# Chunked attention with a router: V in runs of two rows, pipeline units of four heads by half a sequence, bf16 turns, earlier q and k

## The chip, the cores and the metric

The kernel runs on one core of a Trainium2 chip. The metric is the device time of one execution in microseconds; lower is better. The core's engines are TensorE (PE in the profile; its weight loads are PEld), VectorE (DVE), ScalarE (ACT), GpSimd (POOL) and SyncE (SP). Each works through its own instructions in order, and semaphores tie them together. Sixteen DMA engines move data between the device memory, where the inputs lie, and the on-chip memory (SBUF). TensorE writes its results to a second on-chip memory (PSUM), from which DVE and ACT read them.

## The reference

Two parts are computed in a row. First attention over chunks of 32 queries. Each chunk sees 16 keys to its left, its own 32 and 8 to its right (56 in all), and 8 memory keys of its head: 64 columns.

```python
batch, n_heads, seq, head_dim = (4, 8, 768, 64)     # q, k, v: float32
...
for c in range(nc):                                  # nc = 768 // 32 = 24
    l_start = max(0, c_start - left_ctx); r_end = min(S, c_end + right_ctx)
    k_full = np.concatenate([mem_k, k[:, :, l_start:r_end]], axis=2)
    v_full = np.concatenate([mem_v, v[:, :, l_start:r_end]], axis=2)
    scores = scale * np.matmul(q_c, k_full.transpose(0, 1, 3, 2))
    a = np.exp(scores - np.max(scores, axis=-1, keepdims=True))
    a = a / (np.sum(a, axis=-1, keepdims=True) + 1e-09)
    out[:, :, c_start:c_end] = np.matmul(a, v_full)
```

The output, as 3072 rows of 512, goes through a mixture of 8 experts. Noisy logits choose two experts for each row, and each expert is a ReLU layer of 512 x 1024 x 512.

```python
noisy_logits = x @ w_gate + np.log1p(np.exp(x @ w_noise)) * noise
top2 = np.argpartition(-noisy_logits, 2, axis=1)[:, :2]
...
h = np.maximum(x[mask] @ w1[e], 0.0)
out[mask] += top2_w[mask, k, None] * (h @ w2[e])
```

## The kernel before

**Tiling.** The 32 heads are taken in 8 groups of four (`GP` = 2 pairs), and a group in two pipeline units. A unit is one pair of heads over the whole sequence of 768, that is six blocks of 128 queries (`BT` = 6); there are 16 units (`NPAIR`).

**Loads.** `load_qk` (L104) brings q and k of a group to SBUF and casts them to bf16. A partition holds six neighbouring rows of each head. `load_v` (L111) brings V already cut into windows: partition j of a head's half holds row j of every chunk's window, so that one piece of the transfer is one row of 64 values. The two heads of a pair lie in the upper and lower 64 partitions and in different columns of `vg`, with zeros elsewhere, which DVE writes first (L130). All these transfers are issued on POOL's queue. There are three buffers of each kind. Memory V goes straight into `memv` (L165), whose extra columns of ones make the row sums.

**A unit's steps.** `qkT_pe` (L206) turns q and k, so that the head dimension lies on the partitions: 12 + 12 matmuls against an identity into four float32 tiles in PSUM, and four ACT copies (L218) that put the rows back in order. `scores_pe` (L223) makes 12 matmuls with the memory keys (L230), 48 with the chunk windows (L240) and 4 that fill what lies beyond the sequence's ends (L243). `max_dve` and `sub_dve` (L249, L254) take the maximum and subtract it on DVE, and ACT takes the exponential (L258). `PT_pe` and `PT_dve` turn the probabilities (L265, L270). `PV_pe` (L273) multiplies them with `memv` (6 matmuls, L279) and with the windows of V (24, L282). `mult_dve` divides by the row sums (L293, L294) into `xrow`. `xT_pe` (L303, L305) turns the result, and `logits_pe` (L313) forms the router's logits.

**Order.** The order of the instructions on each engine is the order of the code. In iteration i of the main loop (L462) stand the P turns of unit i-1, logits of i-3, the maximum of i, turns of q and k of i+2, the P copy of i-1, subtraction and exponential of i, P·V of i-1, scores of i+1, the division of i-1 and the x turns of i-2. After these come the loads of the group two ahead, in every second iteration, and one step of the routing (`route`, L320) of a finished batch, which is mostly DVE work. A step of it writes the batch's rows to device memory (L385) from one of two `xrow` buffers. The first expert weights are loaded on POOL's queue in iteration 11.

**PSUM.** The turned q, k, P and x share three PSUM tiles of one tag (`tr`); the scores, the P·V result and the logits have their own.

After attention, indices are made, rows gathered in buckets of 128, and the experts run (L644, L652) to the end.

Of the kernel before, what the change touches and what calls it, by code (L numbers as in the profile page):

```python
# [12 lines left out]
F32 = mybir.dt.float32  # L13
# [11 lines left out]
def kernel(  # L25
# [28 lines left out]
    WIN = left_ctx + chunk + right_ctx  # L54
    CTX = WIN + n_mem
    SJ = S // 128
    assert D == 64 and CTX == 64 and 4 * chunk == 128 and S == 128 * SJ
# [17 lines left out]
    xd_part = dram_disjoint_views(xd, B + 1)  # L75
# [8 lines left out]
    def body():  # L84
# [12 lines left out]
        vbufs = [ap_.tile([128, GP, ncnk, 2, D], BF16, name=f"vg{i}", bufs=1) for i in range(3)]  # L97
# [13 lines left out]
        def load_v(g, i=None):  # L111
            vg = groups[g][2]
            for x in range(GP) if i is None else (i,):
                for hh in range(2):
                    p0, hd = 64 * hh, 2 * (GP * g + x) + hh

                    def piece(c, n, j=0, nj=WIN):
                        nc.gpsimd.dma_start(  # L118
                            out=vg[p0 + j:p0 + j + nj, x, c:c + n, hh, :],
                            in_=bass.AP(v.tensor, v.offset + (hd * S + c * chunk + j - left_ctx) * D, [[D, nj], [chunk * D, n], [1, D]]))  # L120

                    first, last = hd == 0, hd == B * H - 1
                    if first:
                        piece(0, 1, left_ctx, WIN - left_ctx)
                    if last:
                        piece(ncnk - 1, 1, 0, WIN - right_ctx)
                    piece(int(first), ncnk - first - last)
# [22 lines left out]
        for b in range(B):  # L150
            nc.scalar.dma_start(out=mk_nat[b * n_mem:(b + 1) * n_mem], in_=mem_k[b].rearrange("h m d -> m h d"))
        wgn_f = rp.tile([128, KP, 2, E], F32, name="wgn_f")
# [5 lines left out]
        OW = D + 2  # L158
        memv = ap_.tile([128, NPAIR, 2, OW], BF16, name="memv", bufs=1)
        nc.vector.memset(memv, 0.0)  # L160
        for hh in range(2):
            nc.vector.memset(memv[64 * hh:64 * hh + 64, :, hh, D:D + 1], 1.0)
        load_qk(0, 1)
        for hh in range(2):
            nc.gpsimd.dma_start(  # L165
                out=memv[64 * hh + WIN:64 * hh + CTX, :, hh, 0:D],
                in_=bass.AP(mem_v.tensor, mem_v.offset + hh * n_mem * D, [[D, n_mem], [2 * n_mem * D, NPAIR], [1, D]]))
        load_v(0, 1)
# [29 lines left out]
        for hp in range(HP):  # L198
            nc.tensor.transpose(out=p_m[:, hp, :], in_=mk_nat[:, 2 * hp:2 * hp + 2, :].rearrange("p h d -> p (h d)"), identity=ident)
# [6 lines left out]
        def qkT_pe(n):  # L206
            g, i = divmod(n, GP)
            qg, kg, _ = groups[g]
            SH = SJ // 2
            for nm, src in (("qT", qg), ("kT", kg)):  # L210
                dst = ap_.tile([128, 128, SJ], BF16, name=nm, bufs=3)
                for x in range(2):
                    p_t = psT.tile([128, SH, 128], F32, name="p_t", tag="tr")
                    for j in range(SH):
                        for hh in range(2):
                            nc.tensor.matmul(out=p_t[64 * hh:64 * hh + 64, j, :], lhsT=src[:, 2 * i + hh, (SH * x + j) * D:(SH * x + j + 1) * D],  # L216
                                             rhs=identb, start=True, stop=True)
                    nc.scalar.copy(dst[:, :, SH * x:SH * (x + 1)], p_t.rearrange("d j p -> d p j"))  # L218
                st[n][nm] = dst.rearrange("d p j -> d (p j)")

        UB = BT // 2

        def scores_pe(n):  # L223
            b, hp = divmod(n, HP)
            qT, kT = st[n]["qT"], st[n]["kT"]
            ps = psS.tile([128, 2, 512], F32, name="ps_s")
            for u in range(BT):
                for hh in range(2):
                    hs = slice(64 * hh, 64 * hh + 64)
                    nc.tensor.matmul(out=ps[:, hh, u * CTX + WIN:(u + 1) * CTX], lhsT=qT[hs, 128 * u:128 * (u + 1)],  # L230
                                     rhs=mkT[hs, hp, b * n_mem:(b + 1) * n_mem], start=True, stop=True)
            for c in range(ncnk):
                u, r = divmod(c, 4)
                for hh in range(2):
                    hs = slice(64 * hh, 64 * hh + 64)
                    lo = left_ctx if c == 0 else 0
                    hi = WIN - right_ctx if c == ncnk - 1 else WIN
                    k0 = chunk * c - left_ctx
                    o = ps[32 * r:32 * r + 32, hh, u * CTX:u * CTX + WIN]
                    nc.tensor.matmul(out=o[:, lo:hi], lhsT=qT[hs, chunk * c:chunk * (c + 1)], rhs=kT[hs, k0 + lo:k0 + hi], start=True, stop=True)  # L240
                    for a, z in ((0, lo), (hi, WIN)):
                        if z > a:
                            nc.tensor.matmul(out=o[:, a:z], lhsT=onesb[hs, :chunk], rhs=neg[hs, :z - a], start=True, stop=True)  # L243
# [571 lines left out]
```

## Time and profile before

| | |
|---|---|
| median of 3 runs | 388.63 us (386.53 to 389.42) |
| span of the profiled execution | 393.1 us |
| the profiled execution's own time beside that span | not given separately |
| instructions | 9217 |
| PE busy | 304.5 us (77%), 4042 matmuls, 4060 weight loads |
| DVE busy | 169.9 us (43%) |
| ACT busy | 119.8 us (30%) |
| POOL busy | 124.5 us (32%) |
| DMA | 83324 packets, 42.93 MB written |

The profile is of one execution. Its span runs from the first to the last instruction and is 4.5 us above the median of the runs. A busy share is an average over the whole span. Attention, routing and experts have different limits, so the stretches are read one by one. In the chain of work that ended last, each step is traced back to what released it. "Issue" there is time in which an engine waited for nothing that the profile shows. In the view by stretches, the columns after the stretch are its length, the busy time of each engine with its number of instructions, the granted share of TensorE's clock, the busy share of the DMA engines, and GB/s written.

### The profile page before, as it was taken

The page shows a single profiled execution, that of the slowest core. Times are in us where ns is not written, and L with a number is a line of the kernel's source. Part 1 is how long each engine was busy: PE and PEld are TensorE (multiplying, and loading weights), DVE is VectorE, ACT ScalarE, POOL GpSimd, SP SyncE. Part 2 cuts the span into 40 slices and gives each one's busy share as a digit, 9 for nine tenths or more (in the row PEclk, how much of TensorE's full clock was granted, in tenths as well). Part 3 has the DMA queues.
Part 4 walks back from the last instruction along what each step waited for, and adds up shares of the span by engine and source line. Part 5 has one row for each costly group of instructions (what it writes and reads, how often), then busy time and mean ns, then how long its engine had stood idle before and what let it go on. Part 6 is the DMA issues. An engine that isn't in the chain of part 4 may idle for free.

```text
span 393.1 us, 9217 instructions
## 1 busy us (share of the span) xinstructions
PE 304.5 (77%) x4042; PEld 188.6 (48%) x4060; DVE 169.9 (43%) x350; ACT 119.8 (30%) x235; POOL 124.5 (32%) x143
## 2 busy tenths in 40 slices
PE   0448688676846433888998998999998999999990
PEld 0436566454634322654465474454454454544540
DVE  7426345787757761342142242241433242443340
ACT  1436354565532200222333232233221312302200
POOL 7766234265000026352100420520605123032061
PEclk9999555898885655699999999999999999999997
DMA  9999999999970412849700291291492921811021
GB/s 92 100 164 156 158 152 94 167 150 141 211 154 3 143 46 80 151 82 216 141 0 2 45 221 30 64 209 34 97 213 88 191 56 71 132 67 70 3 115 59
DMA packets 83324, 42.93 MB, mean 109 GB/s; under 512 B 57255, under 2 KB 76711, under 8 KB 83280
## 3 DMA queue, kind: packets, MB, share of 16 engines
q0 software_dynamic: 74928, 38.85, 70.6%
q1 hardware_dynamic: 8064, 3.38, 3.4%
q8 instruction: 34, 0.56, 0.6%
q10 hardware_dynamic: 288, 0.07, 0.1%
q14 instruction: 10, 0.08, 0.1%
HBM read 61.32 MB, written 10.65 MB: 183 GB/s over the span
## 4 chain that ended last, share of the span: by engine, by line
PE 60%; DVE 15%; issue 10%; DMA 7%; ACT 3%; POOL 3%; POOLq 0%; DVEq 0%; ACTq 0%
PE ps_h L644 24%; PE ps_y L652 21%; DMA x_rows<-xrow 4%; PE p_t L216 3%; DMA kg<-in_k_dram 2%; PE ps_o L279 2%; PE ps_o L282 2%; DVE xrow L294 2%; PE p_t L589 2%; DVE vg L130 2%; DVE xTb L590 2%; POOL out_dram L660 2%; DVE mx L251 1%; ACT qT L218 1%; PE p_x L303 1%
## 5 line engine op out<-in xcount | busy, mean ns | idle before, releaser
L644 PE MATMUL ps_h<-xTb,w1t 128*128 128x512 bf16 (+3 forms) x608 | 107.8, 328 | 1.1 <-DVE xTb L590 1.0
L652 PE MATMUL ps_y<-w2t,ht 128*128 128x512 bf16 x430 | 98.9, 379 | 1.0 <-issue 0.2
L644 PEld LDWEIGHTS <-w1t 128*128 128x128 bf16 x864 | 64.7, 98 | 45.0 <-issue 1.1
L632 DVE TENSOR_SCALAR ht<-ps_h 128x416 bf16<-128x416 f32 (+2 forms) x68 | 41.7, 613 | 81.0 <-PE ps_h L644 81.0
L660 POOL DMA_INDIRECT out_dram<-acc,sidx x28 | 28.0, 998 | 144.9 <-DVE acc L659 142.4
L652 PEld LDWEIGHTS <-ht 128*128 128x128 bf16 x448 | 42.3, 98 | 48.9
L630 ACT ACTIVATE ht<-ps_h 128x416 bf16<-128x416 f32 (+2 forms) x68 | 36.3, 535 | 87.2 <-PE ps_h L644 83.1
L580 POOL DMA_INDIRECT xl<-x_rows,gidx x28 | 29.1, 1038 | 71.4 <-DVE ov1b L523 48.4
L644 PE MATMUL ps_h<-xTs,w1t 128*128 128x32 bf16 x256 | 45.4, 177 | 0.2 <-DVE xTs L605 0.2
L118 POOL DMA_DIRECT2D vg<-in_v_dram x34 | 32.9, 974 | 35.4 <-PE ps_o L282 29.8
L656 ACT ACTIVATE acc<-ps_y,meta 128x512 f32<-128x512 f32 x28 | 19.2, 687 | 76.5 <-PE ps_y L652 47.7
L659 DVE SCALAR_TENSOR_TENSOR acc<-ps_y,meta,acc 128x512 f32<-128x512 f32 x28 | 21.0, 751 | 38.6 <-PE ps_y L652 38.6
L590 DVE COPY xTb<-p_t 128x512 bf16<-128x512 bf16 x28 | 11.8, 423 | 27.1 <-PE p_t L589 26.9
L218 ACT CAST qT<-p_t 128x384 bf16<-128x384 f32 x32 | 16.9, 586 | 20.2 <-PE p_t L216 20.2
L216 PE MATMUL p_t<-identb,kg 128*64 128x128 bf16 x192 | 14.1, 275 | 10.5 <-ACT qT L218 7.7
L251 DVE TENSOR_REDUCE mx<-ps_s 128x12 f32<-128x768 f32 x16 | 15.2, 950 | 12.1 <-PE ps_s L243 12.1
L305 ACT COPY xt<-p_x 128x768 bf16<-128x768 bf16 x16 | 12.8, 799 | 22.5 <-PE p_x L303 22.5
L216 PE MATMUL p_t<-identb,qg 128*64 128x128 bf16 x192 | 11.5, 265 | 9.5 <-DMA qg<-in_q_dram 5.1
L279 PE MATMUL ps_o<-memv,PT 128*128 128x132 bf16 x96 | 11.2, 273 | 9.4 <-DVE PT L270 9.4
L589 PE MATMUL p_t<-identb,xl 128*128 128x128 bf16 x112 | 11.2, 224 | 8.9 <-DVE xTb L590 8.9
L218 ACT CAST kT<-p_t 128x384 bf16<-128x384 f32 x32 | 17.0, 597 | 2.0 <-PE p_t L216 1.7
L294 DVE TENSOR_TENSOR xrow<-ps_o,rec 128x768 bf16<-128x768 f32 x16 | 15.3, 958 | 5.3 <-DMA x_rows<-xrow 4.8
(128 smaller groups left out, 295.5 us busy)
## 6 DMA issues: line engine op xcount, KB each, us to landing
w1t<-in_moe_w_dram POOLq DMA_DIRECT2D x8, 1024.0 KB
w2t<-in_moe_w_dram POOLq DMA_DIRECT2D x8, 1024.0 KB
vg<-in_v_dram POOLq DMA_DIRECT2D x30, 168.0 KB
x_rows<-xrow SPq DMA_DIRECT2D x3, 792.0 KB, 6.3
qg<-in_q_dram POOLq DMA_DIRECT2D x6, 384.0 KB
kg<-in_k_dram POOLq DMA_DIRECT2D x6, 384.0 KB
qg<-in_q_dram POOLq DMA_DIRECT2D x4, 192.0 KB
kg<-in_k_dram POOLq DMA_DIRECT2D x4, 192.0 KB
```

The costliest lines, as they stand in the source:

```text
L118: nc.gpsimd.dma_start(out=vg[p0 + j:p0 + j + nj, x, c:c + n, hh, :], in_=bass.AP(v.tensor, v.offset + (hd * S + c * chunk + j - left_ctx) ...
L216: nc.tensor.matmul(out=p_t[64 * hh:64 * hh + 64, j, :], lhsT=src[:, 2 * i + hh, (SH * x + j) * D:(SH * x + j + 1) * D], rhs=identb, start= ...
L218: nc.scalar.copy(dst[:, :, SH * x:SH * (x + 1)], p_t.rearrange("d j p -> d p j"))
L294: nc.vector.tensor_tensor(out=xr, in0=po.rearrange("p x (u h) c -> p x u h c", h=2)[:, :, :, :, :D], in1=rec.rearrange("p x (u h o) -> p x ...
L580: nc.gpsimd.indirect_dma_start(out=xl, out_offset=None, in_=xd, in_offset=bass.IndirectOffsetOnAxis(ap=gidx[:, p:p + 1], axis=0), bounds_c ...
L590: nc.vector.tensor_copy(xTv[:, :, p, :], p_t)
L630: nc.scalar.activation(out=dst, in_=src, func=Act.Relu)
L632: nc.vector.tensor_scalar(out=dst, in0=src, scalar1=0.0, scalar2=None, op0=Alu.max)
L644: nc.tensor.matmul(out=ps_h[:, o:o + w], lhsT=w1t[:, kp, f * 128:(f + 1) * 128], rhs=rhs(kp), start=(kp == 0 and i == 0), stop=(kp == KP - ...
L652: nc.tensor.matmul(out=ps_y, lhsT=ht[:, f, j * CAP:(j + 1) * CAP], rhs=w2t[:, f, :], start=(f == 0), stop=(f == FB - 1))
L659: nc.vector.scalar_tensor_tensor(out=a, in0=ps_y, scalar=gate, in1=a, op0=Alu.mult, op1=Alu.add)
L660: nc.gpsimd.indirect_dma_start(out=out_part[p], out_offset=bass.IndirectOffsetOnAxis(ap=sidx[:, p:p + 1], axis=0), in_=a, in_offset=None, ...
```

## The change

A unit is now all four heads of a group over half of the sequence: three blocks of 128 queries, 12 chunks. There are still 16 units, two to a group.

**V.** A partition holds two neighbouring rows of a window, so that a piece of the transfer is 128 values instead of 64. The four heads lie in four quarters of 28 partitions each (`QW` = 32, of which 4 are for memory). Even and odd rows are separate columns e = 0, 1. Scores, probabilities and memory keys are ordered alike: a head's 64 columns become two runs of 32, and k is read with a step of two.

**P·V.** The four heads' probabilities for one e fill the 128 partitions. Each half of them (64 rows, two heads) is multiplied by itself: 12 matmuls with `memv` and 48 with V, instead of 6 and 24 over 128 rows.

**Turns.** q and k are turned with transposes into bf16, one PSUM tile and one ACT copy of 768 columns each. The copies have four buffers instead of three.

**Memory V.** Four float32 loads on SP's queue bring it into `mv_nat`, which DVE clears first, and two ACT copies with a mask as scale (`mine`) place it in `memv`.

**Order.** q and k of group 0 are loaded whole, and its V afterwards. q and k of a group are issued one group earlier than before; V stays. The turns of q and k stand three units ahead instead of two, and the logits behind them. Rows of the last batch are written in other pieces. The number of the score, P-turn, x-turn and logits matmuls of a unit does not change, nor do the shapes of DVE's work.

```diff
+    WP = WIN // 2
+    QW = 32
...
-        vbufs = [ap_.tile([128, GP, ncnk, 2, D], BF16, name=f"vg{i}", bufs=1) for i in range(3)]
+        vbufs = [ap_.tile([128, ncnk, 2, 2, D], BF16, name=f"vg{i}", bufs=1) for i in range(3)]
...
+            for hd in range(2 * GP):
+                p0, x, gh = QW * hd, hd % 2, 2 * GP * g + hd
+                def piece(c, n, j=0, nj=WP):
+                    nc.gpsimd.dma_start(
+                        out=vg[p0 + j:p0 + j + nj, c:c + n, x, :, :].rearrange("p c e d -> p c (e d)"),
+                        in_=bass.AP(v.tensor, v.offset + (gh * S + c * chunk + 2 * j - left_ctx) * D, [[2 * D, nj], [chunk * D, n], [1, 2 * D]]))
...
-        load_qk(0, 0)
+        load_qk(0)
...
-        load_v(0, 0)
...
+        mv_nat = ap_.tile([128, NG, 2, D], F32, name="mv_nat", bufs=1)
+        nc.vector.memset(mv_nat, 0.0)
+        mine = ap_.tile([128, 2], F32, name="mine", bufs=1)
+        for hd in range(2 * GP):
+            for hh in range(2):
+                nc.vector.memset(mine[QW * hd:QW * hd + QW, hh:hh + 1], float(hd % 2 == hh))
+            nc.sync.dma_start(out=mv_nat[QW * hd + WP:QW * hd + QW].rearrange("p g e d -> p g (e d)"), ...)
...
+        load_v(0)
         for hh in range(2):
-            nc.gpsimd.dma_start(out=memv[64 * hh + WIN:64 * hh + CTX, :, hh, 0:D], ...)
-        load_v(0, 1)
+            nc.scalar.activation(out=memv[:, :, :, hh * D:hh * D + D], in_=mv_nat, func=Act.Copy, scale=mine[:, hh:hh + 1])
...
-                dst = ap_.tile([128, 128, SJ], BF16, name=nm, bufs=3)
-                for x in range(2):
-                    p_t = psT.tile([128, SH, 128], F32, name="p_t", tag="tr")
-                    ... nc.tensor.matmul(out=p_t[64 * hh:64 * hh + 64, j, :], lhsT=src[:, 2 * i + hh, ...], rhs=identb, start=True, stop=True)
-                    nc.scalar.copy(dst[:, :, SH * x:SH * (x + 1)], p_t.rearrange("d j p -> d p j"))
+                dst = ap_.tile([128, 128, SJ], BF16, name=nm, bufs=4)
+                p_t = psT.tile([128, SJ, 128], BF16, name="p_t", tag="tr")
+                for j in range(SJ):
+                    for hh in range(2):
+                        nc.tensor.transpose(out=p_t[64 * hh:64 * hh + 64, j, :], in_=src[:, 2 * hh + i, j * D:(j + 1) * D], identity=identb)
+                nc.scalar.copy(dst, p_t.rearrange("d j p -> d p j"))
...
+                    nc.tensor.matmul(out=o[:, :, lo:hi], lhsT=qT[:, chunk * c:chunk * (c + 1)],
+                                     rhs=kT[:, k0 + 2 * lo:k0 + 2 * hi].rearrange("d (i e) -> d e i", e=2), start=True, stop=True)
...
+            for e in range(2):
+                for x in range(CB):                       # CB = 12 chunks of the half
+                    u, r = divmod(x, 4)
+                    for s in range(2):
+                        ss = slice(64 * s, 64 * s + 64)
+                        nc.tensor.matmul(out=pv[32 * r:32 * r + 32, s, u, :2 * D], lhsT=PT[ss, 2 * u + e, 32 * r:32 * r + 32],
+                                         rhs=vg[ss, CB * half + x, :, e, :], start=False, stop=(e == 1), skip_group_check=True)
...
         qkT_pe(0)
+        qkT_pe(1)
         scores_pe(0)
-        qkT_pe(1)
+        qkT_pe(2)
         for i in range(NPAIR + 3):
             if 0 <= i - 1 < NPAIR:
                 PT_pe(i - 1)
+            if i < NPAIR:
+                max_dve(i)
+            if i + 3 < NPAIR:
+                qkT_pe(i + 3)
             if 0 <= i - 3 < NPAIR:
                 logits_pe(i - 3)
...
-            if i % GP == 0 and i // GP >= 1 and i // GP + 2 < NG:
-                g = i // GP + 2
-                new_group(g)
-                ...
+            if i % GP == 0:
+                g = i // GP + 3
+                if 3 <= g - 1 < NG:
+                    load_v(g - 1)
+                if g < NG:
+                    new_group(g)
+                    load_qk(g)
```

More of the change, by code (lines that the diff above doesn't have):

```diff
@@ L238, in scores_pe @@
+            for c in range(CB * half, CB * half + CB):
+                u, r = divmod(c - CB * half, 4)
+                for hh, x, hs, qT, kT, mT in heads:
+                    lo = left_ctx // 2 if c == 0 else 0
+                    hi = WP - right_ctx // 2 if c == ncnk - 1 else WP
                     k0 = chunk * c - left_ctx
[L239 to L240 removed]
@@ L305, in xT_pe @@
+            for u in range(UB):
+                for s in range(2):
+                    nc.tensor.transpose(out=p_x[:, u, s, :], in_=xrows[b][:, UB * half + u, 128 * y + 64 * s:128 * y + 64 * s + 64].bitcast(BF16), identity=identb)
+            xt = ap_.tile([128, UB, 2, 128], BF16, name="xt")
             nc.scalar.copy(xt, p_x)
```

166 lines of the change are left out of this document (75 added, 91 removed).

## The prediction

> **What bounds the kernel now.** First the page's forty slices (9.83 us each), which say where the change can act.
>
> ```profile
> span 393.1 us, 9217 instructions
> ...
> PEclk9999555898885655699999999999999999999997
> DMA  9999999999970412849700291291492921811021
> ```
>
> The expert part, from 157.7 us on (the last row of the chain below), runs at full TensorE clock and is not edited; only attention and routing before it can move. In them the DMA engines look full for eleven slices and the TensorE clock falls to half in slices 5 to 7 and again later. Two suspects, then. The chain of work that ended last, read in order of time (start, length, what), tells them apart:
>
> ```profile
> 15.98 9.09 DMA kg<-in_k_dram
> ...
> 26.73 0.71 ACT P L258
> ...
> 30.48 0.78 PE ps_o L279 x6
> ...
> 43.96 0.26 PE ps_s L230 x12
> ...
> 46.74 1.10 issue
> 47.84 1.17 PE p_t L216 x18
> ...
> 49.58 0.78 PE ps_o L279 x6
> 50.36 0.76 PE ps_o L282 x21
> 51.12 0.26 PE ps_s L230 x12
> ...
> 78.29 0.45 PE ps_o L279 x6
> ...
> 89.23 0.45 PE ps_o L279 x6
> ...
> 100.86 14.07 DMA x_rows<-xrow
> ...
> 157.69 6.34 PE ps_h L644 x32
> ```
>
> Up to about 40 us the chain runs through landings: k of group 1 lands at 25.1, and ACT, which works in order, does unit 0's exponentials only behind the copies made from it. After that it is a loop of engines. Score blocks start at 43.96 and 51.12, so a unit takes 7.16 us at half clock; P·V starts at 78.29 and 89.23 two units apart, so 5.5 us at full clock. One half-clock unit is read straight off the rows: 1.10 "issue", 1.74 turns of q and k (47.84 to 49.58), 1.54 P·V, and the rest scores, x and P turns and logits. Late in attention a store of x rows takes 14.07 us. The next view (stretch; busy us of PE, PEld, DVE, ACT, POOL; clock; DMA share; GB/s) gives the rates:
>
> ```profile
> 13.00:15.00 2.00, 1.79 (x36) 1.49 (x35) 0.00 (x0) 1.80 (x5) 2.00 (x3) 1.00 0.34 19
> 20.00:22.00 2.00, 0.00 (x0) 0.00 (x0) 0.00 (x0) 0.00 (x0) 2.00 (x3) 1.00 1.25 183
> 24.00:27.00 3.00, 1.65 (x76) 1.36 (x76) 0.17 (x1) 1.66 (x4) 1.95 (x3) 1.00 2.59 145
> ...
> 74.40:94.90 20.50, 13.92 (x456) 11.11 (x454) 16.47 (x40) 12.13 (x21) 12.85 (x16) 1.00 1.54 154
> 101.70:115.40 13.70, 8.62 (x285) 6.57 (x284) 7.37 (x20) 7.83 (x14) 0.00 (x0) 1.00 1.08 210
> ```
>
> By the order of issue, 20 to 22 us moves q and k (183 GB/s written) and 24 to 27 us moves V (145). From 13 to 15 us DMA nearly stops (19). In the long full-clock stretch DVE is busy 16.47 of 20.5 us: a full-clock unit is nearly DVE's, and the change leaves DVE's per-unit shapes alone.
>
> **V and the order of loads.**
>
> ```profile
> vg<-in_v_dram POOLq DMA_DIRECT2D x30, 168.0 KB
> ...
> qg<-in_q_dram POOLq DMA_DIRECT2D x6, 384.0 KB
> ...
> nz_all<-in_moe_noise_dram SPq DMA_DIRECT2D x1, 96.0 KB, 6.0
> ...
> wgn_f<-in_moe_w_gate_dram SPq DMA_DIRECT2D x1, 16.0 KB, 2.0
> ```
>
> A group of four heads has four V loads, 688 kB, 4.75 us at 145 GB/s, and 786 kB of q and k, 4.3 us at 183. Half as many V pieces of twice the length move the same bytes. Bounds: no gain (4.75 us), or q and k's rate (3.75 us). I take 4.3, halfway, since 256 B written is nearer the old 128 B than q's 768 B but the count halves: 0.45 us a group. It counts only while landings set the pace, three groups: 1.3 us (0 to 3).
>
> The load order: q and k of all four heads, then V, so the hole at 13 to 15 us goes, worth about 1.8 us (2.00 x (1 - 19/183)); POOL no longer waits for DVE's memset of memv (L160). The noise load, now on SP behind the memory-V loads, moves from an idle stretch into this one: minus 0.5, up to 2. Against it, turns now run three units ahead, not two: k of group 2 is needed a unit earlier, and TensorE, in order, holds P·V of unit 0 and the scores behind it. If k of group 1 lands near 22 and a group takes 8.6 to 9, k of group 2 lands at about 31, when unit 0's P·V began at 30.4. So most of the 3 us is eaten; a later group is covered, because its q and k are issued a group sooner and only V waits for P·V. Net at the start: -1 (+3 to -4).
>
> **The start on the engines.**
>
> ```profile
> 12.04 0.17 DVE L178 CAST ident<-identb 32x32 f32<-32x32 bf16 x1
> ...
> L160 DVE MEMSET memv<- 128x1056 uint32 x1 | 0.9, 938 | 0.2 <-issue 0.2
> ...
> L550 DVE MEMSET quarter<- 32x1 f32 x4 | 0.2, 59 | 0.1
> ```
>
> TensorE's first work waits for ident. DVE gains a memset of mv_nat (1024 words, 0.91 us by L160), eight small ones (0.47) and two more on memv (0.1): ident at 13.6. SP's four memory-V loads wait for that memset (about 11.6) and, by the 2.0 to 6.0 us of SP's first loads, land at 13.6 to 17.6. Two ACT copies of 1024 columns follow ahead of all of ACT's other copies; scaled from L305 below, 1.07 us each. Then mkT, four q and k copies, scores of unit 0, four copies, and exp of unit 0 at about 25 against 26.7 now. The cover is the landing of k of group 1 near 22: if memory V lands at 17.6, exp slips past 26.7 by 2 or 3. I take nothing for it.
>
> **The turns.** (Line, engine, tiles, count | busy, mean ns | idle before.)
>
> ```profile
> L218 ACT CAST kT<-p_t 128x384 bf16<-128x384 f32 x32 | 17.0, 597 | 2.0 <-PE p_t L216 1.7
> L305 ACT COPY xt<-p_x 128x768 bf16<-128x768 bf16 x16 | 12.8, 799 | 22.5 <-PE p_x L303 22.5
> ...
> PEld L313 <- ACT xt L305: 8.9, 13, 1.2
> ```
>
> 24 turns stay 24. ACT's four copies of 597 ns become two like L305: 2.39 to 1.60 us a unit; if the strided read costs twice the old copy, 2.39 and nothing. q and k now need two PSUM tiles, not four, of the three, so TensorE waits less for ACT: the turns take 1.74 of which about 0.3 is such waiting. Logits go behind the turns, which covers most of the wait for xt (8.9 us over 13 times in PEld): 0.2 to 0.5 a unit. DVE-bound units keep none of it.
>
> **P·V and scores.**
>
> ```profile
> PE 304.5 (77%) x4042; PEld 188.6 (48%) x4060; DVE 169.9 (43%) x350; ACT 119.8 (30%) x235; POOL 124.5 (32%) x143
> ...
> q8 instruction: 34, 0.56, 0.6%
> ...
> L240 PE MATMUL ps_s<-kT,qT 64*32 64x56 bf16 (+2 forms) x768 | 9.5, 209 | 0.6 <-ACT kT L218 0.6
> ```
>
> P·V grows from 6+24 matmuls over 128 rows to 12+48 over 64. The scores already run 48 such half-height ones in 9.5/16 = 0.59 us of 56 columns, so halves do run beside each other; with 128 columns I expect the old 1.54 at half clock, +0.1 (upper bound, no overlap of halves: +1.5). Scores keep 64 matmuls; a two-element stride in k: +0.0 to 0.2. The q8 row (packets, MB, share) is instructions: 0.56 MB over 8102 TensorE instructions is 69 B each, 16.5 kB a packet, so a packet feeds some 239. By the code a unit has 24 turns and 64 score, 6 P-turn, 30 P·V, 6 x-turn and 6 logits matmuls, each with its load: 272 instructions, and 332 after. That adds 960 in all, four packets. The chain's "issue" piece (1.10) waits for nothing that the profile shows, and a unit's instructions fill about one packet, so I read it as that supply: +0.25 a unit, for 0.25 packets more. Half-clock unit: -0.3 -0.2 +0.1 +0.25 = about -0.15; over some eight such units -1 (+5 to -4).
>
> **The x row store.**
>
> ```profile
> POOL xl L580 <- DVE ov1b L523: 48.4, 1, 48.4
> ...
> DVE xrow L294 <- DMA x_rows<-xrow: 4.8, 2, 4.0
> ```
>
> mult of unit 12 reuses the buffer of batch 1 and waits for its store, which queues beside expert weights that in turn follow V and q, k of group 7. With those q and k gone earlier (2 to 4 us of DMA), the weights end sooner: -1.5 (0 to -4). The last batch's store comes in three pieces rather than two; the gathers wait for DVE's index work (first row), not for stores: 0.
>
> Sum: -1 -1 -1.5 = -3.5 us on the profiled execution, whose span of 393.1 stands 4.5 above the median of 388.63 (its own run time is not given beside the span); I carry the difference over: **385.1**.
>
> [...] The first row below is the last stretch at half clock before the clock was full; the second and third rows are the x and P turns alone (PE, then the engine that reads them).
>
> ```profile
> 64.20:67.60 3.40, 3.40 (x106) 2.88 (x104) 1.84 (x5) 1.76 (x4) 1.68 (x2) 0.50 0.18 14
> ...
> 64.20:67.60 3.40, 0.82 (x6) 0.41 (x1) 0.50 0.18 14
> ...
> 64.20:67.60 3.40, 0.66 (x6) 0.00 (x0) 0.50 0.18 14
> ```
>
> ```profile
> 67.60:71.00 3.40, 1.04 (x24) 0.74 (x24) 3.16 (x9) 1.26 (x4) 1.80 (x3) 1.00 1.67 106
> ```
>
> TensorE was busy all 3.40 us, 1.48 of it in transposes, and the clock then stood at 1.00. [...]
>
> **The rivals.**
> 1. Faster: the clock opens early. Fewer waits inside a unit make a 3.4 us stretch without a hole likelier, as at 64.2. The four half-clock units between 44 and 71 then run at 5.5 instead of 7.16: -6.6 more, **378.5**. Against: the "issue" holes remain.
> 2. The change doesn't bring what it says: V moves at its old rate, early landings are eaten by the longer lead, and DVE hides the rest: 0 to -1, **388**.
> 3. Slower: instruction supply. P·V becomes as dense a stream as the scores, so TensorE runs dry sooner. If every hole is 1.8 us instead of 1.1, that is 4 x 1.8 + 16 x 0.7 = 18.4 us; half of the units have DVE's work as cover, which leaves 9.2: -3.5 + 9.2 = +5.7, **394.3**. For it: the 1.10 us hole above. Against: DVE's 16.47 of 20.5 us in the full-clock stretch, which is cover. It decides once the added holes exceed 3.5 + 3.9 = 7.4 us.
> [...]
> 5. Slower: memory V lands at 17.6, ACT's copies and unit 0 start 3 us later, nothing behind absorbs it, and the strided k costs its 0.2 in half the units: +3 + 1.6, **393.2**.
>
> **How the numbers follow.** A measurement of this kernel can tell about 1% (3.9 us) from no change. Forecast (380 to 388) 0.45, of which 0.27 lies below 384.7; rival 1 0.15; rival 2 0.15; rival 3 0.12, rival 4 0.07, rival 5 0.06. Faster by over 1%: 0.27 + 0.15 = 0.42; within: 0.18 + 0.15 = 0.33; slower: 0.25. The range runs from rival 1 with the start at its best (-3 more) to rival 4: 375 to 395.
>
> **What would show it.** Right: q8 at 38 packets; no stretch near 19 GB/s before 30 us; ACT's q and k copies near 0.8 us each; "issue" before logits' loads gone; V's stretch above 145 GB/s; P·V pairs no longer than 1.6 us at half clock; the x row wait below 4.0. Wrong: exp of unit 0 after 28 us, issue holes over 1.5 us, P·V over 2 us, or a clock that stays at half past 75 us.

## Result, and the profile after

The change makes the kernel slower: 391.87 us median (391.09 to 393.95, four runs) against 387.58 us (385.69 to 389.42, four runs) of the kernel before on the same chip, a ratio of **1.0111** with a 95% interval of 1.0062 to 1.0161. A second measurement, on another chip, gave 1.0104 (1.0053 to 1.0154). The forecast was 385.1 us, so its direction was wrong. That 391.87 us lies between the stated 375 and 395 says little, since they reach from a faster rival to a slower one.

The page of the kernel after, execution of 391.09 us:

```profile
span 389.4 us, 10191 instructions
...
PE 304.5 (78%) x4534; PEld 190.5 (49%) x4552; DVE 171.1 (44%) x361; ACT 113.8 (29%) x205; POOL 113.0 (29%) x137
...
PEclk9996887896666555889999999999999999999997
DMA  8999796996992412889600390390592921712021
...
q8 instruction: 37, 0.61, 0.6%
```

TensorE is busy as long as before (304.5 us), ACT 6 us less, and the clock is fuller between 40 and 60 us, though lower from 88 to 110 (0.69 against 0.84). No engine is busy for more than 1.9 us longer, and still the time went up. The two spans must not be set against each other, because they differ in a part that the change does not touch. From the first gather of rows to the first expert matmul it is 13.8 us in the profile before (143.9 to 157.7), 6.3 in that of the kernel after (147.5 to 153.8) and 13.7 in a second profile of the kernel after (148.1 to 161.8). In between stand 96 small matmuls of the routing (`ps_w`), which take 1.0 us in the one and 7.9 in the others, with "issue" holes among them.

```profile
L580 POOL DMA_INDIRECT xl<-x_rows,gidx x10: 1007/1012/1158, 143.9 to 165.0; - x10
```
```profile
L605 POOL DMA_INDIRECT xl<-x_rows,gidx x11: 1007/1012/1176, 147.5 to 163.3; - x11
...
L568 PE MATMUL ps_w<-ovc,sone x96: 164/172/188, 149.3 to 150.1; 128*32 128x2 bf16 x96
```
```profile
L605 POOL DMA_INDIRECT xl<-x_rows,gidx x9: 1007/1012/1139, 148.1 to 163.1; - x9
...
L568 PE MATMUL ps_w<-ovc,sone x96: 163/172/187, 150.8 to 158.5; 128*32 128x2 bf16 x96
```

(View of one tile's instructions; before, after, after a second time: durations in ns, then first and last start.) The difference goes with the chip and not with the kernel. Over the fourteen profiles of this text the way takes 6.2 to 6.3 us in the four that are known to come from one chip and in the first of the kernel after; it takes 13.6 to 13.8 us in the eight from three other chips and in the first of the kernel before. What stalls the small matmuls there is open. The first gather, ahead of all this, is the mark that tells: 3.6 and 4.2 us later than before, about the 4.3 us by which the medians differ. The place to look is attention. The same view of the sixteen exponentials, first and last start, of the kernels before and after:

```profile
L258 ACT ACTIVATE P<-sd x16: 835/844/884, 26.6 to 126.2; 128x768 bf16<-128x768 f32 x16
```
```profile
L270 ACT ACTIVATE P<-sd x16: 827/843/877, 29.2 to 129.3; 128x768 bf16<-128x768 f32 x16
```

Unit 0 starts 2.6 us later and unit 15 3.1 later. Between them a unit takes 99.6/15 = 6.64 us before and 100.1/15 = 6.67 after: what the new unit should have saved is not there. The waits of TensorE that the profile can put down to nothing ("issue": us in total, times, longest) show what came in its place. First before, then after, both from 12 to 142 us:

```profile
PE p_t L216 <- issue: 3.6, 2, 2.5
PE p_x L303 <- issue: 1.3, 1, 1.3
PE p_p L265 <- issue: 1.2, 1, 1.2
...
```
```profile
PE ps_s L251 <- issue: 8.0, 5, 3.7
PE p_t L221 <- issue: 5.6, 2, 3.1
PE p_p L277 <- issue: 2.7, 1, 2.7
PE ps_s L242 <- issue: 1.5, 1, 1.5
PE ps_o L300 <- issue: 1.2, 2, 1.0
...
```

In all, 6.3 us have become 19.2. They are at no one place of the code: scores, turns, P turns, P·V. The late start itself is in the waits and in ACT's timeline of the kernel after:

```profile
ACT memv L174 <- DMA mv_nat<-in_mem_v_dram: 17.7, 1, 17.7
...
PE p_t L221 <- ACT mkT L207: 5.5, 1, 5.5
```
```profile
19.77 2.19 ACT L174 ACTIVATE memv<-mv_nat,mine 128x1024 bf16<-128x1024 f32 x2 [17.68 <-DMA mv_nat<-in_mem_v_dram]
```

Memory V, issued at about 12 us, is there at 19.8. ACT waits 17.7 us for it; the copy of the turned memory keys (mkT) and those of q and k queue behind on ACT, and TensorE waits 5.5 us for the PSUM tile that mkT's copy frees.

### The profile page after: what moved, and what is told of

Its sections match the earlier page's. It is cut to its first block, busy times and chain, and to the rows that moved or that the text cites. A ratio compares the mean times of both kernels' runs of the same rounds, so it can differ in the third digit from the quotient of the medians.

```text
span 389.4 us, 10191 instructions
## 1 busy us (share of the span) xinstructions
PE 304.5 (78%) x4534; PEld 190.5 (49%) x4552; DVE 171.1 (44%) x361; ACT 113.8 (29%) x205; POOL 113.0 (29%) x137
## 5 line engine op out<-in xcount | busy, mean ns | idle before, releaser
L669 PE MATMUL ps_h<-xTb,w1t 128*128 128x512 bf16 (+3 forms) x608 | 108.9, 329 | 1.1 <-DVE xTb L615 1.0
L605 POOL DMA_INDIRECT xl<-x_rows,gidx x28 | 29.2, 1041 | 65.7 <-DVE srank L555 47.8
L681 ACT ACTIVATE acc<-ps_y,meta 128x512 f32<-128x512 f32 x28 | 19.2, 687 | 75.4 <-PE ps_y L677 60.8
L119 POOL DMA_DIRECT2D vg<-in_v_dram x34 | 25.4, 759 | 54.0 <-PE ps_o L300 48.9
L294 PE MATMUL ps_o<-memv,PT 64*128 64x130 bf16 x192 | 11.2, 270 | 12.4 <-DVE PT L282 12.4
L614 PE MATMUL p_t<-identb,xl 128*128 128x128 bf16 x112 | 11.2, 225 | 8.6 <-DVE xTb L615 6.8
L251 PE MATMUL ps_s<-kT,qT 64*32 64x56 bf16 (+2 forms) x768 | 11.4, 203 | 8.3 <-issue 8.0
L222 ACT COPY qT<-p_t 128x768 bf16<-128x768 bf16 x16 | 12.8, 798 | 15.1 <-PE p_t L221 15.1
L270 ACT ACTIVATE P<-sd 128x768 bf16<-128x768 f32 x16 | 13.6, 847 | 9.1 <-DVE sd L268 9.1
## 6 DMA issues: line engine op xcount, KB each, us to landing
w2t<-in_moe_w_dram POOLq DMA_DIRECT2D x8, 1024.0 KB, 17.6
```

The costliest lines, as they stand in the source:

```text
L119: nc.gpsimd.dma_start(out=vg[p0 + j:p0 + j + nj, c:c + n, x, :, :].rearrange("p c e d -> p c (e d)"), in_=bass.AP(v.tensor, v.offset + (gh ...
L270: nc.scalar.activation(out=P.rearrange("p x h c -> p h x c"), in_=sd.rearrange("p h (x u) (e c) -> p (h x) (u e) c", x=2, e=2), func=Act.E ...
L605: nc.gpsimd.indirect_dma_start(out=xl, out_offset=None, in_=xd, in_offset=bass.IndirectOffsetOnAxis(ap=gidx[:, p:p + 1], axis=0), bounds_c ...
L669: nc.tensor.matmul(out=ps_h[:, o:o + w], lhsT=w1t[:, kp, f * 128:(f + 1) * 128], rhs=rhs(kp), start=(kp == 0 and i == 0), stop=(kp == KP - ...
L681: nc.scalar.activation(out=accs[acc[p]], in_=ps_y, func=Act.Copy, scale=gate)
```

## Experiments

The theories at the start: **A**, TensorE's instruction supply (332 instructions a unit instead of 272); **B**, the late start by memory V; **C**, the longer lead of the turns (three units). Later ones are named where they come up. All ratios are to the kernel before on the same chip.

**1. The kernel before again** (`before_again`), no edit.

> The kernel before, unchanged, profiled a second time. Theory A (instruction supply): TensorE's 'issue' holes in attention sum to some 6 us in the first profile of before and 18 us in that of after; here 4 to 9 us again. Theory B (late memory V) says nothing of it. The first profile of before had 13.8 us from the first gather to the first ps_h, that of after 6.3; if that was a chance of one execution, it is 6 to 8 us here and the span 385 to 388. Ratio 1.00 within 0.5%.

Measured: 0.9985 (0.9947 to 1.0024). Its holes in TensorE are again 6.2 us in all, so 6 us is no accident of one profile. A miss: the way from the first gather to the first expert matmul is again 13.7 us and the span 393.5, where 6 to 8 and 385 to 388 were expected if that way was a chance of one execution.

**2. Memory V first** (`a_memv_first`), theory B, on the kernel after.

```diff
+        mv_nat = ap_.tile([128, NG, 2, D], F32, name="mv_nat", bufs=1)
+        nc.vector.memset(mv_nat, 0.0)
...
+            nc.sync.dma_start(
+                out=mv_nat[QW * hd + WP:QW * hd + QW].rearrange("p g e d -> p g (e d)"),
...
         for vb in vbufs:
             nc.vector.memset(vb, 0.0)
```

> After, with mv_nat cleared and its four loads issued ahead of the V buffers' clearing. Theory B (the start is lost to memory V, whose loads issued at 11.7 us land at 19.8): memV's ACT copies start near 13, exp of unit 0 at 24 to 25.5 instead of 29.2, and the end moves by -3 to -5 us, to a ratio of 1.000 +- 0.004 to before. Theory A (instruction supply sets the middle): the start moves likewise, but less than half of it arrives at the end, ratio 1.005 to 1.011.

Measured: 1.0043 (1.0008 to 1.0077). The first exponential comes at 24.8 us, 1.8 before that of the kernel before, and the last one at 128.2, still 2.0 after it:

```profile
L270 ACT ACTIVATE P<-sd x16: 826/845/866, 24.8 to 128.2; 128x768 bf16<-128x768 f32 x16
```

So the late start is real and worth some 0.7% (1.0111 less 1.0043; the kernel after did not run on this chip), but not the whole: of 4.4 us gained at the first unit 1.1 are left at the last. The ratio lies between those that B (up to 1.004) and A (from 1.005) had named. A unit takes 6.89 us here.

**3. P·V in 60 matmuls, in the kernel before** (`b_pv60`), theory A alone: each matmul of P·V is split by columns, one for each head.

```diff
-                nc.tensor.matmul(out=pv[32 * r:32 * r + 32, u // UB, u % UB, :, :D], lhsT=PT[:, u, 32 * r:32 * r + 32],
-                                 rhs=vg[:, i, c], start=False, stop=True, skip_group_check=True)
+                for hh in range(2):
+                    nc.tensor.matmul(out=pv[32 * r:32 * r + 32, u // UB, u % UB, hh, :D], lhsT=PT[:, u, 32 * r:32 * r + 32],
+                                     rhs=vg[:, i, c, hh], start=False, stop=True, skip_group_check=True)
...
```

> Before, with each P.V matmul cut into two of half the columns: 60 instead of 30 a unit, the same columns in all, the same result, 332 instead of 272 TensorE instructions a unit as in after. Theory A: 'issue' holes grow to 12 to 18 us and the time by 3 to 7 us, ratio 1.008 to 1.018; q8 37 to 38 packets. Theory B, or any theory in which loads or the start set it: ratio 1.000 to 1.004.

Measured: **1.0188** (1.0118 to 1.0258). Of the groups of instructions between 12 and 142 us, those of P·V in the kernel before and then here, and the "issue" waits here:

```profile
L282 PE MATMUL ps_o<-vg,PT 128*32 128x128 bf16 x384 | 11.3, 271 | 0.2 <-issue 0.2
L279 PE MATMUL ps_o<-memv,PT 128*128 128x132 bf16 x96 | 11.2, 273 | 9.4 <-DVE PT L270 9.4
```
```profile
L284 PE MATMUL ps_o<-vg,PT 128*32 128x64 bf16 x768 | 12.6, 226 | 2.3 <-issue 2.3
L280 PE MATMUL ps_o<-memv,PT 128*128 128x66 bf16 x192 | 11.7, 225 | 4.7 <-DVE PT L270 4.7
```
```profile
PE ps_s L240 <- issue: 9.5, 5, 3.7
PE ps_o L284 <- issue: 2.3, 2, 1.8
PE p_t L216 <- issue: 2.2, 2, 1.2
...
```

P·V itself grew by 1.8 us in all, while 1.88% is 7.4 us. The same work in more instructions costs what the change costs and more, with nothing else of the change there. The holes, 14.9 us in all, turn up mostly at the scores, which were not touched.

**4. Turns two units ahead, after the logits, in the kernel after** (`a_look2`), theory C.

```diff
-        qkT_pe(2)
...
-            if i < NPAIR:
-                max_dve(i)
-            if i + 3 < NPAIR:
-                qkT_pe(i + 3)
             if 0 <= i - 3 < NPAIR:
                 logits_pe(i - 3)
...
+            if i < NPAIR:
+                max_dve(i)
+            if i + 2 < NPAIR:
+                qkT_pe(i + 2)
```

> After, with the turns two units ahead instead of three and the logits ahead of them, as in before. Theory C (the longer lead makes the start wait for a later group of q and k): exp of unit 1 moves from 35.9 to about 33 and the end by -1 to -3 us. Theory A and B: no gain, since q and k of groups 1 and 2 had landed by 18.9 and 29.3; the logits' wait for xt comes back, +0 to +3 us.

Measured: 1.0154 (1.0093 to 1.0214). The first two exponentials come 1.4 and 1.2 us earlier than in the kernel after (27.8 and 34.7), but the last one 1.0 later (130.3). The longer lead is not what costs; C falls.

**5 to 7. Three parts of the change on the kernel before**: the bf16 turns with one copy each (`b_turns`); q and k issued one group sooner in the main loop (`b_order`); both, and the logits behind the turns (`b_both`, and once more as `b_both_again`). D is the loss by the turns, E the loss by V that lands late.

```diff
-                for x in range(2):
-                    p_t = psT.tile([128, SH, 128], F32, name="p_t", tag="tr")
...
+                p_t = psT.tile([128, SJ, 128], BF16, name="p_t", tag="tr")
+                for j in range(SJ):
+                    for hh in range(2):
+                        nc.tensor.transpose(out=p_t[64 * hh:64 * hh + 64, j, :], in_=src[:, 2 * i + hh, j * D:(j + 1) * D], identity=identb)
+                nc.scalar.copy(dst, p_t.rearrange("d j p -> d p j"))
```
```diff
-            if i % GP == 0 and i // GP >= 1 and i // GP + 2 < NG:
-                g = i // GP + 2
-                new_group(g)
...
+            if i % GP == 0:
+                g = i // GP + 3
+                if 3 <= g - 1 < NG:
+                    load_v(g - 1)
+                if g < NG:
+                    new_group(g)
+                    load_qk(g)
```

> The kernel before with one part of the change: q and k turned by transposes into bf16, one PSUM tile and one ACT copy of 768 columns each instead of two float32 tiles and two copies. Instructions per unit stay at 272. Theory A (the change loses by TensorE's instruction supply): nothing lost here, holes of TensorE that wait for nothing stay near 6 us in all between 12 and 142 us, ACT saves 0.8 us a unit, ratio 0.990 to 1.000. Theory D (the change loses by its turns, transposes or the strided ACT read): ratio above 1.005, and it appears here already.

> The kernel before with one other part of the change: after the start, q and k of a group are issued one group sooner on POOL's queue, ahead of nothing but behind the V of the group before; turns stay two units ahead. Theory A: holes near 6 us, the x row store of batch 1 leaves sooner and DVE's wait for it (4.8 us in the profile before) falls under 2, ratio 0.992 to 1.000. Theory E (V now lands late because q and k go ahead of it, and this is a part of the loss): V's landing waits appear on TensorE, ratio 1.003 to 1.010.

> The kernel before with three parts of the change together: bf16 turns with one copy each, q and k issued a group sooner, and the logits behind the turns. P·V keeps 30 matmuls a unit over 128 rows, memory V its old road. Theory A: this is the change without its price: holes near 6 us, ratio 0.985 to 0.995. If the loss sits in the turns or in the order, ratio 1.003 or more.

> The same three parts (bf16 turns, q and k a group sooner, logits behind the turns) on the kernel before, measured once more beside the kernel after. By the page budget of TensorE's instructions: 272 a unit, ratio 0.990 to 0.998 to the kernel before, 1.1 to 1.8% under the kernel after. If the three parts bring nothing: 0.998 to 1.003.

Measured: turns 0.9972 (0.9937 to 1.0006); order 1.0006 (0.9970 to 1.0041); together 0.9955 (0.9909 to 1.0001), and the second time **0.9954** (0.9918 to 0.9989), which is 1.5% under the kernel after beside it (1.0104). D falls, since it needed more than 1.005 for the turns. E needed 1.003 to 1.010 for the order; 1.0006 speaks against it, and no wait of TensorE for V stands in that profile. `b_both` just misses the 0.985 to 0.995 that were expected. Another miss: in `b_order` DVE still waits 4.6 us for the x row store, where under 2 was expected.

```profile
DVE xrow L294 <- DMA x_rows<-xrow: 4.6, 2, 3.8
```

A third miss counts for more. In `b_both`, with 272 instructions, the holes were expected near 6 us, and its first profile has 16.1:

```profile
PE p_t L214 <- issue: 6.1, 2, 3.3
PE ps_s L237 <- issue: 5.0, 4, 2.6
PE ps_s L227 <- issue: 2.0, 1, 2.0
PE p_x L300 <- issue: 1.2, 1, 1.2
PE p_p L262 <- issue: 1.1, 1, 1.1
PE ps_o L279 <- issue: 0.7, 2, 0.4
```

**8. Half of P·V left out, in the kernel after** (`a_pv30`).

```diff
-            for e in range(2):
+            for e in range(1):
                 for x in range(CB):
...
```

> The kernel after with the odd rows of the windows (e = 1) left out of P·V: 6 + 24 half-height matmuls a unit instead of 12 + 48, so 272 instructions a unit as before; everything else of the change stays, late memory V too. This leaves out half of P·V's sum. Theory A (instruction supply): the instruction row falls to about 33 packets, the holes from 18 us to 6 to 8 us between 12 and 142 us, and the ratio to 0.990 to 1.000, of which the shorter P·V itself (0.5 to 0.8 us a unit where TensorE sets the pace) is a part. Theory B (the loss is the late start by memory V alone): the holes and about 1.007 to 1.011 remain, since the start is unchanged.

Measured: 0.9835 (0.9771 to 0.9899). The time fell further than expected, but TensorE's work fell with the instructions, and the holes did not go to 6 to 8 us: they are 16.6. So A in its first form, holes that go with the number of instructions, is wrong. A hole is not a price for each instruction.

**What the holes have in common.** Counted along TensorE's records of matmuls and weight loads, the holes of all kernels up to 138 us stand at numbers 445, 701, 957, 1213 and so on, always a multiple of 256 apart (give or take one where the two kinds overlap), and every packet of the instruction row q8 is 16 kB (37 packets, 0.61 MB): 64 B for each of 256 instructions, called a page of instructions from here on. Two stretches of the kernel after, from one such border to the next, and the hole behind one of them (stretch; PE, PEld, DVE, ACT, POOL busy; clock; DMA share; GB/s):

```profile
50.22:52.71 2.49, 2.45 (x128) 2.02 (x128) 0.49 (x2) 2.12 (x3) 0.30 (x1) 1.00 1.28 191
52.72:55.60 2.88, 0.00 (x0) 0.00 (x0) 0.69 (x1) 0.11 (x1) 2.88 (x5) 1.00 1.13 129
91.00:94.17 3.17, 3.13 (x128) 2.37 (x128) 0.68 (x2) 1.89 (x4) 0.49 (x1) 0.50 0.05 10
```

In the first two rows 128 matmuls and 128 loads run dry in 2.49 us, and then comes nothing for 2.88. The third row, at half clock and beside idle DMA queues (share 0.05), takes 3.17 us, and the hole behind it is 0.60. When was the next packet moved? The DMA queues of this stretch, from the border to 53.20 and from there to 53.40:

```profile
q0 software_dynamic: 736, 0.54, 122.2%
```
```profile
...
q8 instruction: 1, 0.02, 30.5%
```

The page for the instructions after 52.7 is fetched only from 53.28 us on, 3.0 after the page before it was entered (50.25), while 736 data packets moved, and 2.34 after that TensorE goes on (55.62). Read in this way over all profiles up to 108 us, a fetch begins a median of 1.05 us after its page's predecessor was entered where DMA was idle in between (43 borders with a share under 0.12) and 3.27 us where it was busy (156 borders with a share over 1; a tenth of them over 4.2). From the last fetch before a border to the first instruction behind it lie at least 2.18 us at 213 of 215 borders. This is **theory F**: a page of 256 instructions is not worked off before the next one has been fetched, so that by these medians it takes at least some 3.4 us beside idle DMA queues (1.05 + 2.3) and 5.6 us beside busy ones (3.27 + 2.3); what the kernel needs less than that stands as a hole. It is an estimate and no constant: single pages behind which TensorE ran dry beside busy queues took from 3.5 to 8.2 us. A unit of 272 instructions is 1.06 pages, by the estimate 6.0 us where DMA is busy throughout; one of 332 is 1.30 pages, 7.3 us. **Theory G**: each packet stalls TensorE by a fixed time.

**9 and 10. Both kernels without the loads of groups 3 to 7** (`b_noload`, `a_noload`). Every engine's instructions but the DMA issues stay; later units compute on the tiles of groups 0 to 2.

```diff
-                new_group(g)
...
+                groups[g] = groups[g - 3]
```

> The kernel before without the loads of q, k and V for groups 3 to 7: these units compute again on the tiles of groups 0 to 2, so every engine has the same instructions, and DMA is nearly idle from about 40 us to the first expert weights. The pages of 256 TensorE instructions (272 a unit, 5.5 to 7 us): theory F (the next page is asked for about 1.1 us after the last one was entered while DMA is idle, and 2 to 5 us after while it is busy, and is there 2.3 us after that; what the unit does faster than this is a hole): between 45 and 90 us fetches start 1.0 to 1.3 us after their page's border, and no hole over 0.3 us is left there (the profile before has three: 1.10, 1.21, 1.30). Theory G (a packet costs TensorE a fixed stall, whatever DMA does): the holes stay at 1 to 1.3 us each. Time: ratio 0.975 to 0.995 by F, landings no longer waited for included.

> The kernel after without the loads of q, k and V for groups 3 to 7, as in the kernel before without them; 332 instructions a unit. Theory F: between 45 and 85 us the fetches start 1.0 to 1.3 us after their page's border and the holes there (2.47, 2.92, 1.49 in the profile after) are gone or under 0.5 us each; against the kernel before without these loads the attention part then loses only the late start (2 to 3 us) and may win some of it back, so that the two ratios differ by less than 0.008. Theory G: the holes stay near 2 us each, and the two ratios differ by 0.011 or more, as the kernels with their loads do.

Measured: 0.9811 (0.9708 to 0.9914) for the kernel before without these loads, 0.9811 (0.9732 to 0.9890) for the kernel after without them. **The loss of 1.1% is gone:** the second against the first of these eight runs gives 0.9987, with a 95% interval of 0.990 to 1.007. The weights' loads move forward, so DMA is idle only from about 48 us on in `a_noload` and from about 54 in `b_noload`; a_noload's page from 52.44 on:

```profile
52.44:54.96 2.52, 2.52 (x128) 2.08 (x128) 1.32 (x3) 2.11 (x3) 0.00 (x0) 0.97 0.03 7
```
```profile
55.90 0.25 PE L251 MATMUL ps_s<-kT,qT 64*32 64x56 bf16 x12 [0.94 <-issue]
```

The same dense page as at 50.22 above; the fetch begins at 53.57, 1.13 after the border instead of 3.0, and the hole is 0.94 instead of 2.9. From there on its fetches begin 0.75 to 1.6 us after their borders, up to 95 us. The "issue" waits of a_noload from 45 to 92 us, where the kernel after has the four holes of 2.47, 2.92, 1.49 and 3.09 us:

```profile
PE ps_s L251 <- issue: 2.1, 2, 1.2
PE ps_o L300 <- issue: 0.8, 2, 0.4
PE p_t L221 <- issue: 0.5, 1, 0.5
```

G would have kept them near 2 us each. Not all went as written: single holes of 0.9 and 1.2 us remain where a page is dense, more than the 0.5 expected. The kernel before without the loads keeps holes of 0.6 at 48.3 and 2.2 at 52.6, where the weights still moved. And the start up to 45 us, where the loads of groups 0 to 2 and the weights run, still has its holes. That start settles something else: in `a_noload` POOL runs no instruction from the border at 37.96 us on, and the next fetch still begins only 3.6 us after it, beside a DMA share of 1.24. So a late fetch goes with the moving data, and does not need POOL to issue any. The sixteen exponentials of b_noload and a_noload:

```profile
L258 ACT ACTIVATE P<-sd x16: 838/844/886, 26.1 to 119.8; 128x768 bf16<-128x768 f32 x16
```
```profile
L270 ACT ACTIVATE P<-sd x16: 827/844/876, 28.7 to 118.0; 128x768 bf16<-128x768 f32 x16
```

6.25 us a unit before, 5.95 after: with quiet DMA queues the changed unit is the faster one, and makes up for its late start in this pair of profiles.

**11. The kernel after again** (`after_again`), beside `b_both_again`.

> The kernel after once more, beside the three parts alone. Ratio 1.008 to 1.015 to the kernel before, and TensorE's holes at page borders again near 18 us in all between 12 and 142 us. If these were an accident of one execution: under 10 us.

Measured: 1.0104 (1.0053 to 1.0154); holes at borders 17.7 us in all.

The fastest of the versions that leave out no work is `b_both`: the kernel before with bf16 turns, q and k a group sooner and the logits behind the turns. Its exponentials, in the two profiles:

```profile
L255 ACT ACTIVATE P<-sd x16: 827/845/857, 26.1 to 118.9; 128x768 bf16<-128x768 f32 x16
```
```profile
L255 ACT ACTIVATE P<-sd x16: 826/845/857, 25.7 to 122.2; 128x768 bf16<-128x768 f32 x16
```

6.19 and 6.43 us a unit, against 6.64 before: near the 6.0 us that the estimate gives for 272 instructions. That would be why it has holes (16.1 us in the first profile): its units come close to that bound, where TensorE in the kernel before waits 7.7 us for ACT's copies of q (none in `b_both`). So a sum of holes is no measure of a loss.

## Why the prediction was wrong

**The step that failed: "a unit's instructions fill about one packet, so I read it as that supply: +0.25 a unit, for 0.25 packets more."** That the hole was instruction supply was right; how it costs, and so the size, was wrong. The term took a packet as a cost of 1.10 us that is paid once for each, and multiplied it by the packets added. In the runs it is a bound on the rate. The 60 instructions more are 0.23 pages, by the estimate above 0.23 x 5.6 = 1.3 us of a unit's least time beside busy DMA queues, where the sum had 0.25. The other terms of that sum, -0.5 a unit for turns and logits, are about what `b_both` shows, 0.2 to 0.45 a unit over all fifteen; in the kernel after nothing of it is left (6.67 against 6.64).

The forecast sum and what the profiles show at the same marks, in us (exponentials of units 0 and 15, first gather; the x row store lies between the exponentials; one profile of each, the last two pairs from one chip each):

| | forecast | after less before | after_again less before_again | a_memv_first less before_again | a_noload less b_noload |
|---|---|---|---|---|---|
| start, to unit 0 | -1 | +2.6 | +3.0 | -1.5 | +2.6 |
| units 0 to 15 | -1 -1.5 | +0.5 | +1.4 | +4.2 | -4.4 |
| unit 15 to first gather | 0 | +0.5 | +0.5 | +0.1 | +0.2 |

In the change as it stands the start is the largest miss. But `a_memv_first` has the early start that was forecast, and then the units lose 4.2 us; `a_noload` has the late start and quiet DMA queues, and the units win 4.4. So while the loads run, the units give back much of an earlier start, and the term for the units is the one that turns the sign.

**Rival 3**, "TensorE runs dry sooner", is what happened, at a chance of 0.12. Its size is luck: it counted 18.4 us of added holes at a fixed 1.8 us for each packet, and 12.9 were added (19.2 less 6.3), at a dozen of the borders, with single holes from 0.2 to 3.7 us. Its sum of +5.7 is near the measured +4.3, which has the late start in it. The sign that was set for being wrong, holes over 1.5 us, was there. Whether DVE's work covered part of the holes, as it held against itself, was not tried.

**"I take nothing for it": the start on the engines.** Memory V was to land between 13.6 and 17.6 us by SP's first loads; it came at 19.8, beside V's transfers, and the first exponential at 29.2, past the mark of 28 that was to show this wrong. Rival 5 had the mechanism (+3 us). Its "nothing behind absorbs it" did not hold: in `a_memv_first` a start 4.4 us earlier leaves 1.1 at unit 15, and the units between take longer (6.89 us), as they would if the page bound held them.

**The turns.** ACT's copies went as worked out, 798 ns against 799 expected:

```profile
L222 ACT COPY qT<-p_t 128x768 bf16<-128x768 bf16 x16 | 12.8, 798 | 15.1 <-PE p_t L221 15.1
```

"Covers most of the wait for xt" is right as well; it stood as 8.9 us in the view of waits and is 3.7 now.

**P·V.** "Halves do run beside each other" is right: P·V's groups are 12.2 and 11.2 us against 11.3 and 11.2, though there are twice as many matmuls.

```profile
L300 PE MATMUL ps_o<-vg,PT 64*32 64x128 bf16 x768 | 12.2, 268 | 1.2 <-issue 1.2
L294 PE MATMUL ps_o<-memv,PT 64*128 64x130 bf16 x192 | 11.2, 270 | 12.4 <-DVE PT L282 12.4
```

**V's rate.** From 45 to 48 us, V alone moves at 160 GB/s against 145 before, which is about the 4.3 us a group that were taken:

```profile
45.00:48.00 3.00, 2.78 (x144) 2.31 (x141) 2.56 (x5) 2.21 (x3) 1.89 (x3) 1.00 1.69 160
```

It buys nothing that the waits show: TensorE waits for V in neither profile.

**The x row store.** The wait fell as forecast, from 4.8 to 0.8 us:

```profile
DVE xrow L313 <- DMA x_rows<-xrow: 0.8, 2, 0.6
```

The reason given, q and k gone earlier, is not confirmed: `b_order` makes this one edit and keeps 4.6. What shortens it was not tried by itself.

**The clock.** The chance of 0.07 for rival 4, and the upper end of the range with it, stand for a clock that stays at half, which no run shows: in the kernel after it steps from 0.50 to 1.00 six times between 42 and 118 us. The stretch ahead of one such step, with the one behind it:

```profile
55.92:59.33 3.41, 3.41 (x52) 3.02 (x54) 2.38 (x3) 2.02 (x3) 1.02 (x2) 0.50 1.49 141
59.33:62.74 3.41, 1.92 (x125) 1.59 (x122) 1.30 (x3) 1.02 (x2) 0.00 (x0) 1.00 1.27 191
```

Of the 3.41 us in the first row, transposes of q, k, x and P fill 2.8, other matmuls alone the remaining 0.6, and the clock stands at 1.00 right after. In the mean the clock is lower than before, though, from 88 to 110 us (0.69 against 0.84; 0.66 against 0.92 in the second profiles), and what that costs was not tried by itself. Two kernels speak against a large cost: `b_order` with a mean clock of 0.90 from 12 to 130 us takes 6.66 us a unit, the kernel before with 0.78 takes 6.64.

**The base.** The sum was made against an execution with a span of 393.1 us and carried over to the median, which was fair for a difference; but the span after (389.4) would have called the change a gain of 3.7 us. Only the medians, and the place of the first gather, show the loss.

**What is open.** Why a fetch begins later beside data, whether its packet queues behind theirs or is asked for later, no run tells; the removal of the loads shows only that they bring it about (3.0 us after its border for the page at 50.22, 1.13 for the same page in `a_noload`). It was not tried, either, what makes single borders free of the delay while the queues are busy. The late start and the page bound are not two terms of the 1.1% that can be added: taking away the one gave 0.7% (`a_memv_first`), the other all of it (no loads).

## What to carry to other kernels

Where TensorE runs many short instructions, count the instructions of a unit in pages of 256 and set them against the unit's time: beside busy DMA queues a page took some 5.6 us here by the medians, and units near that bound took longer with more instructions at nearly the same engine time (`b_pv60`: 60 more a unit, 1.8 us more of P·V in all, 7.4 us more of the kernel's time). A hole put down to "issue" that stands at such a border was here a limit of a rate, not a price: look for what is 256 instructions before it and when the instruction queue moved its packet. And an edit that makes one engine's work shorter (turns) has to be tried without the one that makes another's instruction stream longer (P·V in halves): the first was worth 0.5% with its two companions, and twice as many P·V matmuls (`b_pv60`, there by columns) cost 1.9%.

## What the runs showed of the hardware

TensorE's instructions came in pages of 256 (16 kB a packet, 37 packets in the profile of the kernel after, which has 9086 matmuls and weight loads). The page behind the running one is fetched a median of 1.05 us after the running one was entered where the DMA queues are idle (43 borders with a share under 0.12), and of 3.27 us after where they are busy (156 borders with a share over 1), a tenth of these over 4.2; TensorE goes on no earlier than 2.18 us after the fetch began at 213 of 215 borders. In the kernel after the clock stood at 1.00 from 59.33 to 62.74 us, behind 3.41 us at half clock of which transposes filled 2.8. Leaving out five groups of loads took 1.9% off the kernel before with every engine's instructions unchanged, and took away the difference between the two kernels (0.9987, 0.990 to 1.007). The 96 small matmuls of `ps_w` take 1.0 us on one chip and 7.7 to 7.9 on three others, whichever kernel runs.
